# Attention and two routed expert layers on one core: scores of two head groups in turns, the second expert's weights fetched before the slot table

## The chip, the cores and the metric

One core of a Trainium2 chip runs the whole program in one launch. The metric is the device time of one execution in microseconds (us). Five engines work side by side, each through its own instructions in order: TensorE (PE; its weight loads are PEld), VectorE (DVE), ScalarE (ACT), GpSimd (POOL) and SyncE (SP), which here issues nearly all DMAs.

## The reference

Attention over 4 sequences, 8 heads, 768 positions, 64 dimensions; each query sees the first `n_global` = 8 keys and a causal window of `n_local` = 96, with a per-head distance penalty. Its output, 3072 rows of 512, goes through two layers of 8 experts with one expert per row:

```
scores = q @ k.T / 8 - slope[h] * dist ; a = softmax(where(keep, scores, -1e9)) ; x = a @ v
layer 1: e = argmax(x @ w_gate);             y = p[e] * relu(x @ w1[e]) @ w2[e]
layer 2: e = argmax(y @ w_gate2 + bias[mod]); the same with its own weights
```

Each expert has `w1` of 512x1024 and `w2` of 1024x512 in f32, 4 MB together.

## The kernel before

**Order of work.** Every piece of work is a function put at a time on a list (`Timeline.at`); the list is sorted once when the program is built, and so the order of instructions on each engine is fixed. The times are units of order alone: an attention tile is 4 units, a quarter of an expert slot is 1.

**Attention.** 24 tiles of 128 queries (`u`), 6 per sequence. All f32 operands are split in a high f16 and a low bf16 part, and a product is three matmuls. Heads go in four groups of two (`HEADS`, L237): (0,2) and (4,6) lie in partitions 0 to 63 of the transposed q and k, (1,3) and (5,7) in 64 to 127. For each group `g` come, in order: `score` (L589: 12 matmuls of 64 rows into one PSUM bank of tag A, 6 in the first tile of a sequence), two `rowmax` on VectorE (L608), two `expo` on ScalarE (L620), `etrans` (L625: f32 transposes on TensorE), `e_hi` (ScalarE) and `e_lo` (VectorE), then `pv` (12 matmuls). Tag A has two banks, so scores of one group can be written while those of the other are read. Beside this run the loads and transposes of the next tiles' q and k, and the routing of finished tiles: gate logits, the largest of 8, a position, and an indirect DMA that writes the row into its expert's region (`xs`).

**Expert layers.** Rows are worked in slots of 128 rows of one expert. Each slot has four quarters `p`: `mm1` (24 matmuls), a split of the result on ScalarE and VectorE (`mm1_out`), `mm2` (6 matmuls of 512 columns). At tile 15 the fullest expert is chosen as leader (`choose(0)`); its weights are loaded during the attention and split into f16 and bf16 (`split`: ScalarE L120, VectorE L347), and two slots of its rows start before the routing has ended. After the last tile, VectorE counts all rows and writes a table of slots (`slot_table`, L722): for each slot its base row, whether weights change there, and the next expert (FNXT). SyncE reads it with register loads (`val`, L804). In this input expert 0 leads; slots 0 and 1 finish it, and experts 1 to 7 begin at slots 2, 6, 9, 13, 16, 20 and 24 (counts computed from the reference).

**Weights and branches.** There is one set of f32 staging buffers, `st1[p]` and `st2[p]`. `stage_in` (L332) issues the DMAs; `change` (L892) splits them on ScalarE and VectorE under a branch; `refill` (L899) loads the next expert behind the splits, under a branch of SyncE on FNXT (L905), four pieces per slot. In layer 1, for slots after 17, each piece has a second register and a second branch (L909, FREFB), which loads the leader of layer 2 once the last expert has begun. The first weights after the leader's are loaded when the table is there (L1040). A SyncE branch that is not taken still raises the semaphores of the DMAs that it leaves out, after waiting for their earlier value, so a split of new weights cannot start before SyncE has passed every refill piece placed ahead of it.

Of the kernel before, what the change touches and what calls it, by code (L numbers as in the profile page):

```python
# [38 lines left out]
PICK = (15, 17)  # L39

MORE = (5, 2)
VHI = H * (D + 1)


# [6 lines left out]
}  # L51
ENG = {
    "kh": "P", "vh": "P", "qh": "P", "mh": "P", "ml": "P", "pp": "P", "pf": "V", "po": "V", "wa": "V",
# [47 lines left out]
def kernel(  # L101
# [199 lines left out]
    def constants():  # L301
        nc.vector.tensor_copy(out=rowoff_b, in_=rowoff[0:1, :])
        nc.vector.memset(meta[:, :, 0:NM - E], 0.0)
        nc.vector.memset(meta[:, :, 2:3], 1.0)
        nc.vector.tensor_copy(out=meta[:, :, 1], in_=tok_id)
        nc.vector.tensor_copy(out=mod_f[:, 1], in_=mod_i[:, :, 0])
        nc.vector.tensor_scalar(out=mod_f[:, 0], in0=mod_f[:, 1], scalar1=-1.0, scalar2=1.0, op0=ALU.mult, op1=ALU.add)
        for i in range(2):
            nc.vector.tensor_tensor(out=mod_b[:, i], in0=mod_f[:, i].unsqueeze(2).to_broadcast([128, NU, E]),
                                    in1=bias_sb[:, i].unsqueeze(1).to_broadcast([128, NU, E]), op=ALU.mult)  # L310
        nc.vector.tensor_tensor(out=meta[:, :, NM - E:NM], in0=mod_b[:, 0], in1=mod_b[:, 1], op=ALU.add)
        for m in range(2):
            nc.vector.tensor_copy(out=wg_hl[m][0], in_=wg_sb[m])
            nc.vector.tensor_tensor(out=wg_hl[m][1], in0=wg_sb[m], in1=wg_hl[m][0], op=ALU.subtract)

        nc.vector.tensor_scalar(out=late[:, 0:1], in0=slot_id, scalar1=float(PICK[1] + 1), scalar2=None, op0=ALU.is_equal)
        nc.vector.tensor_scalar(out=late[:, 1:2], in0=slot_id, scalar1=float(PICK[1] + 1), scalar2=None, op0=ALU.is_gt)

    def clear(m, e):

# [174 lines left out]
    def choose(m):  # L495

        cn = counts(m)
        mx = small.tile([128, 8], F32, tag="cmx", name="cmx", bufs=1)
        nc.vector.max(out=mx, in_=cn)
        ix = small.tile([128, 8], U32, tag="cix", name="cix", bufs=1)  # L500
        nc.vector.max_index(out=ix, in_max=mx, in_values=cn)
        nc.vector.tensor_copy(out=lead_f[m], in_=ix[:, 0:1])
        k = lead_k[m]
        ro = small.tile([1, 1], F32, tag="ro", name="ro", bufs=1)
        ts = nc.gpsimd.tensor_scalar
        if m == 0:
# [12 lines left out]
        if m == 1:  # L519
            nc.gpsimd.tensor_copy(out=lead_i[m][:, 3:4], in_=k[0:1, :])  # L520
        lead[m] = [nc.values_load(lead_i[m][0:1, i:i + 1], engines=[ET.SP], min_val=0,
                                  max_val=(E - 1, (E - 1) * REG + 128, E * REG - 128)[i]) for i in range(3)]


    vg_of = {}
# [62 lines left out]

    def score(u, g):  # L589

        d = st[u]
        p0 = 64 * (HEADS[g][0] % 2)
        sp = d["sp", g] = bank("A", "sp").rearrange("p (j c) -> p j c", j=2)
        keys = [(slice(WB - 128, WB), d["kt"], 0)]
        if u % QT:
            keys.append((slice(0, NA), kt_of[u - 1], 128 - LMAX + 1))
        else:
            keys[0] = (slice(0, 128), d["kt"], 0)
        for j, h in enumerate(HEADS[g]):
            for cols, kt, c0 in keys:  # L600
                for n, (x, y) in enumerate(((0, 0), (0, 1), (1, 0))):
                    lq = d["qt"][p0:p0 + 64, x, h // 2, :]
                    rk = kt[p0:p0 + 64, y, h // 2, c0:c0 + cols.stop - cols.start]
                    nc.tensor.matmul(out=sp[:, j, cols], lhsT=lq.bitcast(BF16) if x else lq,  # L604
                                     rhs=rk.bitcast(BF16) if y else rk, start=(n == 0), stop=(n == 2),
                                     skip_group_check=True)

    def rowmax(u, g, j):  # L608

# [107 lines left out]
            wide_attention()  # L717


    FBASE, FCHG, FNXT, FREFB, FCNT, FE1, NF = 0, 1, 2, 3, 4, 5, 6  # L720

    def slot_table(m):  # L722

# [7 lines left out]
        left, fin, lst, f = T("left", 1), T("fin", 1), T("lst", 1), T("f", NF)  # L731
        io = iota8[0:32, :]

        def col(i):
# [34 lines left out]
        def changes():  # L769

            stt(out=tmp, in0=start, scalar=slot_id, in1=sel, op0=ALU.is_equal, op1=ALU.mult)
            stt(out=tmp, in0=tmp, scalar=1.0, in1=not0, op0=ALU.mult, op1=ALU.mult, accum_out=first)
            stt(out=tmp, in0=start, scalar=s_end, in1=some, op0=ALU.is_equal, op1=ALU.mult, accum_out=has)

            stt(out=tmp, in0=tmp, scalar=first, in1=io, op0=ALU.mult, op1=ALU.mult, accum_out=col(FNXT))
            stt(out=tmp, in0=start, scalar=c0, in1=some, op0=ALU.is_equal, op1=ALU.mult)
            stt(out=tmp, in0=tmp, scalar=1.0, in1=io, op0=ALU.mult, op1=ALU.mult, accum_out=col(FE1))
            if m == 0:

                tt(out=fin, in0=col(FCNT), in1=slot_id, op=ALU.is_equal)  # L780
                tt(out=lst, in0=live, in1=has, op=ALU.subtract)
                tt(out=col(FCHG), in0=first, in1=fin, op=ALU.add)
                stt(out=fin, in0=first, scalar=late[:, 1:2], in1=late[:, 0:1], op0=ALU.mult, op1=ALU.add)
                tt(out=col(FREFB), in0=fin, in1=lst, op=ALU.mult)
            else:
                V.tensor_copy(out=col(FCHG), in_=first)
                V.memset(col(FREFB), 0.0)

        def turn():
            tpp = bank("C", "tpp")  # L790
            nc.tensor.transpose(tpp[0:NF, 0:32], f, ident[0:32, 0:32])
            tab[m] = const.tile([NF, 32], I32, name=f"slots{m}")
            V.tensor_copy(out=tab[m], in_=tpp[0:NF, 0:32])
            regs["e1", m] = val(m, FE1, 0, [ET.SP], E - 1)

        return lead_part, starts, bases, changes, turn

# [101 lines left out]
    def refill(m, s, k, i):  # L899

        if k == 0 and i == 0:
            regs["r", m, s] = (val(m, FNXT, s, [ET.SP], E - 1),
                               val(m, FREFB, s, [ET.SP], 1) if m == 0 and s > PICK[1] else None)
        nxt, refb = regs["r", m, s]
        with tc.If(nxt > 0):  # L905
            for p in (2 * k, 2 * k + 1):
                stage_in(p, m, nxt, (i,))
        if refb is not None:
            with tc.If(refb > 0):  # L909
                for p in (2 * k, 2 * k + 1):  # L910
                    stage_in(p, 1, lead[1][0], (i,))
        if k == 1 and i == 1:
            del regs["r", m, s]

# [93 lines left out]
    def refills(tl, m, s, n, t_min=-1e9):  # L1008
        for i in range(2):
            for k in range(2):  # L1010
                tl.at(max(n + MOFF[f"f{i}{k}"], t_min + 0.25 + 0.1 * k + 0.01 * i), lambda k=k, i=i: refill(m, s, k, i))

    def later(f):

        def guard(fn):
# [6 lines left out]
    def slots(tl, m, t0, t_table):  # L1022
# [14 lines left out]
        end = t1 + NP * fixed  # L1037
        assert t1 + MOFF["e1"] > t_table
        for p in range(NP):
            tl.at(t1 + MOFF["e1"] + 0.1 + 0.5 * p, lambda p=p: stage_in(p, m, regs["e1", m]))  # L1040
            for k in range(2):
                tl.at(t1 + MOFF["e1"] + 0.2 + 0.8 * p + 0.3 * k, lambda p=p, k=k: change(m, 0, p, 0, k))
                tl.at(t1 + MOFF["e1"] + 0.8 + 0.9 * p + 0.3 * k, lambda p=p, k=k: change(m, 0, p, 1, k))
# [52 lines left out]
    for u in range(NU):  # L1096
# [11 lines left out]
                       ("wa", lambda u: place_a(0, st[u], eng_of("wa"))), ("place", route_p)):  # L1108
            tl.at(SOFF.get(f"{nm}{u}", n + off_of(u, nm)), lambda u=u, fn=fn: fn(u))
        for g in range(4):  # L1110
            for nm, fn in (("S", score), ("EH", e_hi), ("EL", e_lo), ("PV", pv)):
                tl.at(n + g + OFF[nm], lambda u=u, g=g, fn=fn: fn(u, g))
            for nm, fn in (("R", rowmax), ("X", expo), ("T", etrans)):
                for j in range(2):
                    tl.at(n + g + OFF[f"{nm}{j}"], lambda u=u, g=g, j=j, fn=fn: fn(u, g, j))
# [62 lines left out]
```

## Time and profile before

| | |
|---|---|
| time, median of 3 runs | 887.59 us (887.04 to 899.56) |
| the profiled execution | 892.53 us, span 891.0 us |
| PE / PEld busy | 830.5 us (93%) / 632.3 us (71%) |
| DVE / ACT / POOL busy | 476.9 (54%) / 401.9 (45%) / 305.9 us (34%) |
| attention at its pace, 54.5 to 226 us | PE 168.23 us of 171.50, DVE 153.62, ACT 141.26 |
| first tiles, 22 to 54 us | PE 31.72 us of 32.00, but 275 matmuls against 557 in 34.48 us later |

Times in the trace are us from the start of the span. Attention fills the first quarter, to about 238 us with its last routing; layer 1 runs to about 600 us, layer 2 to the end. Busy times are of instructions as recorded; matmuls overlap, so that a group's busy time is less than count times mean.

### The profile page before, as it was taken

To read this page: it belongs to the slowest core of one execution; us is meant where nothing else is said; L and a number is where in the kernel's file an instruction comes from. 1 tells how busy PE (TensorE), PEld (TensorE's weight loads), DVE (VectorE), ACT (ScalarE), POOL (GpSimd) and SP (SyncE) were. 2 spreads that over 40 slices of the span, in tenths; PEclk is the share of its full clock that TensorE was granted. 3 is DMA by queue.
4 is the path that set the end of the run, shared out by engine and by line. 5 is a ranking of instruction groups with operands and counts; after the bars stand their busy time and mean duration, and the time that the engine had idled before them with its cause. 6 is when DMAs were issued, how large, how long until landed. Compare 5 with 4: busy or idle time off the path is not lost. (4 is left out here: it accounts for less than half of the span.)

```text
span 891.0 us, 30257 instructions
## 1 busy us (share of the span) xinstructions
PE 830.5 (93%) x10153; PEld 632.3 (71%) x10153; DVE 476.9 (54%) x1745; ACT 401.9 (45%) x858; POOL 305.9 (34%) x495
## 2 busy tenths in 40 slices
PE   5999999999688999999999788969999999999995
PEld 4888888888566777677777566647677777777773
DVE  5668898899843747656573634646311125111133
ACT  5568888888513434525341524332222225222242
POOL 6358777785432333423341422102111111111110
PEclk9999999999699999999999899999999999999998
DMA  8657766677249989987887684832562117322200
GB/s 145 177 150 211 181 147 144 155 193 226 66 104 267 248 185 240 221 262 181 248 240 168 148 216 135 213 116 52 150 162 69 52 50 209 78 62 52 51 28 16
DMA packets 227582, 133.99 MB, mean 150 GB/s; under 512 B 177148, under 2 KB 199676, under 8 KB 227360
## 3 DMA queue, kind: packets, MB, share of 16 engines
q1 hardware_dynamic: 220896, 112.10, 51.5%
q0 software_dynamic: 6320, 19.37, 6.2%
q8 instruction: 85, 1.39, 0.7%
q14 instruction: 137, 1.12, 0.4%
q10 hardware_dynamic: 144, 0.00, 0.0%
HBM read 79.54 MB, written 33.77 MB: 127 GB/s over the span
## 5 line engine op out<-in xcount | busy, mean ns | idle before, releaser
L870 PE MATMUL hp<-mx,h 128*128 128x128 f16 x3520 | 326.4, 222 | 9.6 <-ACTq L896 7.7
L870 PE MATMUL hp<-mx,l 128*128 128x128 f16 x1760 | 312.8, 222 | 7.0 <-DVEq L896 3.9
L870 PEld LDWEIGHTS <-h 128*128 128x128 f16 x3520 | 278.9, 99 | 48.7 <-ACTq L896 10.6
L881 DVE SCALAR_TENSOR_TENSOR hl<-hp,hh 128x256 bf16<-128x256 f32 x220 | 93.1, 423 | 268.7 <-ACT hh L880 139.4
L880 ACT ACTIVATE hh<-hp 128x256 f16<-128x256 f32 x220 | 84.2, 383 | 272.0 <-PE hp L870 233.8
L870 PEld LDWEIGHTS <-l 128*128 128x128 bf16 x1760 | 174.6, 99 | 8.8 <-DVEq L896 4.6
L889 PE MATMUL y<-l,hh 128*128 128x512 bf16 x440 | 167.5, 381 | 1.4 <-DVEq L896 1.4
L889 PE MATMUL y<-h,hh 128*128 128x512 f16 x440 | 167.7, 381 | 0.0
L889 PE MATMUL y<-h,hl 128*128 128x512 f16 x440 | 167.3, 380 | 0.0
L347 DVE TENSOR_TENSOR l<-st,h 128x1024 bf16<-128x1024 f32 x88 | 111.9, 1273 | 52.3 <-ACTq L896 25.3
L889 PEld LDWEIGHTS <-hh 128*128 128x128 f16 x880 | 77.4, 98 | 53.3 <-issue 0.8
L120 ACT CAST h<-st 128x1024 f16<-128x1024 f32 x88 | 91.2, 1043 | 50.7 <-SPq L909 20.7
L934 POOL DMA_INDIRECT out_dram<-o,ti x26 | 27.0, 1040 | 227.3 <-ACTq L896 189.9
L479 POOL DMA_INDIRECT xs<-r,posi x29 | 33.3, 1150 | 176.2 <-DVEq L896 61.3
L623 ACT ACTIVATE e<-e,nm 128x232 f32<-128x232 f32 (+1 forms) x192 | 84.0, 470 | 7.3 <-DVE nm L616 5.1
L889 PEld LDWEIGHTS <-hl 128*128 128x128 bf16 x440 | 43.2, 98 | 54.1 <-issue 2.2
L604 PE MATMUL sp<-kt,qt 64*128 64x128 f16 (+3 forms) x1056 | 77.8, 225 | 2.5 <-DVE nm L616 1.9
L604 PEld LDWEIGHTS <-qt 64*128 64x128 f16 (+1 forms) x1056 | 61.8, 101 | 14.5 <-issue 11.1
L616 DVE CUSTOM_DVE_ANT_0 e<-sp,bias_mid 128x232 f32<-128x232 f32 x160 | 61.3, 385 | 5.7 <-PE sp L604 5.6
L646 DVE TENSOR_TENSOR el<-et,eh 128x512 bf16<-128x512 f32 (+1 forms) x96 | 60.9, 634 | 1.7 <-ACT eh L640 1.7
L640 ACT CAST eh<-et 128x512 f16<-128x512 f32 (+1 forms) x96 | 52.4, 546 | 19.0 <-PE et L634 17.3
L634 PE MATMUL et<-ident,e 128*128 128x128 f32 x192 | 50.7, 297 | 1.0 <-ACT e L623 1.0
(201 smaller groups left out, 1138.9 us busy)
## 6 DMA issues: line engine op xcount, KB each, us to landing
st<-in_moe_w_dram SPq DMA_DIRECT2D x88, 512.0 KB
mxf<-xs SPq DMA_DIRECT2D x29, 266.0 KB
x_d<-r SPq DMA_DIRECT2D x29, 256.0 KB
ld_k<-in_k_dram SPq DMA_DIRECT2D x24, 256.0 KB
ld_q<-in_q_dram SPq DMA_DIRECT2D x24, 256.0 KB
ld_v<-in_v_dram SPq DMA_DIRECT2D x24, 256.0 KB
row<-xg SPq DMA_DIRECT2D x24, 256.0 KB
xs<-empty SPq DMA_DIRECT2D x18, 266.0 KB
```

Source lines behind the costliest of these rows:

```text
L120: nc.scalar.copy(out=out, in_=in_)
L347: (nc.vector if engines[i][1] == "V" else nc.gpsimd).tensor_tensor(out=l, in0=w, in1=h, op=ALU.subtract)
L604: nc.tensor.matmul(out=sp[:, j, cols], lhsT=lq.bitcast(BF16) if x else lq, rhs=rk.bitcast(BF16) if y else rk, start=(n == 0), stop=(n == 2 ...
L616: nc.vector.tensor_tensor_reduce(out=d["e", g][:, j, 0:w], in0=d["sp", g][:, j, 0:w], in1=(bias_mid if t else bias_first)[:, HEADS[g][j], ...
L623: nc.scalar.activation(out=e, in_=e, func=ACTF.Exp, bias=d["nm", g][:, j:j + 1], scale=-1.0)
L634: nc.tensor.transpose(tp[:, j, :], e[:, j, NA if t else 0:WB if t else 128], ident)
L640: nc.scalar.copy(out=eh[:, 0:n], in_=d["et", g][:, 0:n])
L646: nc.vector.tensor_tensor(out=el[:, 0:n], in0=d["et", g][:, 0:n], in1=d["eh", g][:, 0:n], op=ALU.subtract)
L870: nc.tensor.matmul(out=hp[:, j, :], lhsT=w[p][:, c, fs], rhs=r.bitcast(BF16) if x else r, start=(n == 0), stop=(n == 11))
L880: nc.scalar.activation(out=hh, in_=hp, func=ACTF.Relu)
L881: nc.vector.scalar_tensor_tensor(out=hl, in0=hp, scalar=0.0, in1=hh, op0=ALU.max, op1=ALU.subtract)
L889: nc.tensor.matmul(out=d["y"], lhsT=d[hx, p][:, j, :], rhs=w[p][:, j, :], start=(p == 0 and j == 0 and i == 0), stop=(p == NP - 1 and j == ...
```

## The change

There are two parts. **Scores**: `score(u, g)` is called for even `g` alone and writes two groups into both banks of tag A, matmul by matmul in turns from partitions 0 to 63 and 64 to 127. The odd group's rowmax goes 0.6 units earlier than before, its expo 0.3. **Weights**: `choose(0)` also writes a guess of the next expert (1 if the leader is 0, else 0), and `stage_in` loads it right behind the leader's splits; when the table is there, a branch per quarter (`first_next`) loads again where the guess was wrong. The second branch of `refill` and its register are gone for slots below AHEAD = 21; from 21 on FNXT = 8 stands for the leader of layer 2, in two branches inside the first.

```diff
+AHEAD = PICK[1] + 4
...
+    "c0s": 1.3, "c1": 15.6, "c1s": 2.0, "rl": 10.6, "oddR": 0.6, "oddX": 0.3, "oddT": 0.0,
...
-        nc.vector.tensor_scalar(out=late[:, 0:1], in0=slot_id, scalar1=float(PICK[1] + 1), scalar2=None, op0=ALU.is_equal)
+        nc.vector.tensor_scalar(out=late[:, 0:1], in0=slot_id, scalar1=float(AHEAD), scalar2=None, op0=ALU.is_equal)
...
+        else:
+            ts(out=lead_i[m][:, 3:4], in0=lead_f[m][0:1, :], scalar1=0.0, scalar2=None, op0=ALU.is_equal)
...
     def score(u, g):
-        p0 = 64 * (HEADS[g][0] % 2)
-        sp = d["sp", g] = bank("A", "sp").rearrange("p (j c) -> p j c", j=2)
+        sp = [bank("A", "sp").rearrange("p (j c) -> p j c", j=2) for _ in range(2)]
+        for i in range(2):
+            d["sp", g + i] = sp[i]
...
-        for j, h in enumerate(HEADS[g]):
+        for j in range(2):
             for cols, kt, c0 in keys:
                 for n, (x, y) in enumerate(((0, 0), (0, 1), (1, 0))):
+                    for i in range(2):
+                        h = HEADS[g + i][j]
+                        p0 = 64 * (h % 2)
...
-                tt(out=col(FREFB), in0=fin, in1=lst, op=ALU.mult)
+                tt(out=fin, in0=fin, in1=lst, op=ALU.mult)
+                stt(out=col(FNXT), in0=fin, scalar=float(E), in1=col(FNXT), op0=ALU.mult, op1=ALU.add)
+                ts(out=spec, in0=lead_f[m][0:32, :], scalar1=0.0, scalar2=None, op0=ALU.is_equal)
+                tt(out=spec, in0=col(FE1), in1=spec, op=ALU.subtract)
+                ts(out=col(FMORE), in0=spec, scalar1=0.0, scalar2=None, op0=ALU.max)
...
     def refill(m, s, k, i):
         if k == 0 and i == 0:
-            regs["r", m, s] = (val(m, FNXT, s, [ET.SP], E - 1),
-                               val(m, FREFB, s, [ET.SP], 1) if m == 0 and s > PICK[1] else None)
+            regs["r", m, s] = val(m, FNXT, s, [ET.SP], E if m == 0 and s >= AHEAD else E - 1)
...
         with tc.If(nxt > 0):
-            for p in (2 * k, 2 * k + 1):
-                stage_in(p, m, nxt, (i,))
-        if refb is not None:
-            with tc.If(refb > 0):
...
+            if m == 0 and s >= AHEAD:
+                with tc.If(nxt < E):
+                    stage(m, nc.s_assert_within(nxt, 0, E - 1, skip_runtime_bounds_check_because="it is under E here"))
+                with tc.If(nxt > E - 1):
+                    stage(1, lead[1][0])
+            else:
+                stage(m, nxt)
...
+    def first_next(m, p):
+        if m == 1:
+            stage_in(p, m, regs["e1", m])
+        else:
+            with tc.If(regs["e1", m] > 0):
+                stage_in(p, m, val(m, FE1, 0, [ET.SP], E - 1))
...
-            tl.at(t1 + MOFF["e1"] + 0.1 + 0.5 * p, lambda p=p: stage_in(p, m, regs["e1", m]))
+            tl.at(t1 + MOFF["e1"] + 0.1 + 0.5 * p, lambda p=p: first_next(m, p))
...
-            for nm, fn in (("S", score), ("EH", e_hi), ("EL", e_lo), ("PV", pv)):
+            if g % 2 == 0:
+                tl.at(n + g + OFF["S"], lambda u=u, g=g: score(u, g))
+            for nm, fn in (("EH", e_hi), ("EL", e_lo), ("PV", pv)):
...
+                    t = n + g + OFF[f"{nm}{j}"] - (OFF[f"odd{nm}"] if g % 2 else 0)
...
+            tl.at(max(MOFF["split0"] + 1.3 * i + p + 1.2, 100 + 0.05 * (2 * p + i)), lambda p=p, i=i: stage_in(p, 0, lead[0][3], (i,)))
```

## Rows read from the trace of the kernel before

**Rows 1.** Busy time of each engine in four full attention tiles; header: columns.

```profile
core 0: us, PE busy (x) PEld busy (x) DVE busy (x) ACT busy (x) POOL busy (x), PEclk, DMA share, GB/s
...
142.34:176.82 34.48, 34.48 (x557) 30.58 (x556) 30.64 (x139) 29.51 (x63) 26.06 (x39) 1.00 0.62 145
```

**Rows 2.** TensorE in order of time: start, us, line, operands, shape, count.

```profile
143.81 0.22 PE L661 MATMUL xp<-vs,eh 128*128 128x65 f16 x2
143.88 0.19 PE L661 MATMUL xp<-vs,el 128*128 128x65 f16 x1
144.00 0.78 PE L604 MATMUL sp<-kt,qt 64*128 64x128 f16 x12
144.71 0.33 PE L633 MATMUL et<-ident,e 128*128 128x128 f32 x1
```

**Rows 3.** Groups by line, same four tiles: count, busy us, mean ns, idle.

```profile
L604 PE MATMUL sp<-kt,qt 64*128 64x128 f16 (+1 forms) x192 | 12.5, 212 | 0.0
L616 DVE CUSTOM_DVE_ANT_0 e<-sp,bias_mid 128x232 f32<-128x232 f32 x32 | 12.3, 385 | 0.0
```

**Rows 4.** TensorE in order of time, the first tiles.

```profile
31.57 1.34 PE L604 MATMUL sp<-kt,qt 64*128 64x128 f16 x12
...
46.52 1.34 PE L604 MATMUL sp<-kt,qt 64*128 64x128 f16 x12
...
54.55 0.33 PE L633 MATMUL et<-ident,e 128*128 128x128 f32 x1
```

**Rows 5.** TensorE in order of time, after its waits; brackets: idle before, releaser.

```profile
265.14 0.27 PE L870 MATMUL hp<-mx,h 128*128 128x128 f16 x2 [0.81 <-DMA mx<-mxs]
...
285.62 0.28 PE L870 MATMUL hp<-mx,h 128*128 128x128 f16 x2 [1.58 <-ACTq L896]
286.90 0.29 PE L870 MATMUL hp<-mx,l 128*128 128x128 f16 x1 [0.99 <-DVEq L896]
...
494.32 0.29 PE L870 MATMUL hp<-mx,h 128*128 128x128 f16 x2 [4.19 <-ACTq L896]
495.59 0.29 PE L870 MATMUL hp<-mx,l 128*128 128x128 f16 x1 [0.99 <-DVEq L896]
...
549.03 0.28 PE L870 MATMUL hp<-mx,h 128*128 128x128 f16 x2 [1.06 <-ACTq L896]
```

**Rows 6.** ScalarE in order of time, weight casts behind their waits.

```profile
284.48 1.04 ACT L120 CAST h<-st 128x1024 f16<-128x1024 f32 x1 [6.88 <-SPq L905]
...
493.17 1.04 ACT L120 CAST h<-st 128x1024 f16<-128x1024 f32 x1 [7.42 <-SPq L909]
...
547.89 1.04 ACT L120 CAST h<-st 128x1024 f16<-128x1024 f32 x1 [4.99 <-SPq L909]
```

**Rows 7.** Busy time of each engine by stretch, columns as in rows 1.

```profile
236.00:256.00 20.00, 15.02 (x174) 11.71 (x174) 15.98 (x84) 3.91 (x11) 5.11 (x7) 0.85 0.11 42
266.00:284.00 18.00, 18.00 (x210) 12.84 (x207) 4.21 (x14) 3.27 (x10) 3.45 (x8) 1.00 1.05 292
287.00:290.00 3.00, 3.00 (x24) 2.52 (x24) 2.42 (x6) 2.47 (x5) 1.86 (x4) 0.51 1.62 160
495.60:501.50 5.90, 5.90 (x39) 3.94 (x40) 4.64 (x11) 5.07 (x9) 1.96 (x4) 0.50 0.49 135
```

**Rows 8.** SyncE queue in order of time: DMA issues.

```profile
266.00 0.39 SPq L334 DMA_DIRECT2D st<-in_moe_w_dram  x1
...
275.04 0.37 SPq L338 DMA_DIRECT2D st<-in_moe_w_dram  x1
...
482.66 1.40 SPq L847 DMA_TRANSPOSE mx<-mxs  x1
486.64 0.36 SPq L940 DMA_DIRECT2D x_d<-r  x1
...
493.14 1.25 SPq L945 DMA_TRANSPOSE x2t<-x_d  x1
```

**Rows 9.** VectorE in order of time, the end of the slot table.

```profile
253.05 0.21 DVE L783 SCALAR_TENSOR_TENSOR tb_fin<-tb_first,late 32x1 f32<-32x1 f32 x1
```

More of the change, by code (lines that the diff above doesn't have):

```diff
@@ L314, in constants @@
             nc.vector.tensor_tensor(out=wg_hl[m][1], in0=wg_sb[m], in1=wg_hl[m][0], op=ALU.subtract)
-        nc.vector.tensor_scalar(out=late[:, 0:1], in0=slot_id, scalar1=float(PICK[1] + 1), scalar2=None, op0=ALU.is_equal)
-        nc.vector.tensor_scalar(out=late[:, 1:2], in0=slot_id, scalar1=float(PICK[1] + 1), scalar2=None, op0=ALU.is_gt)
+        nc.vector.tensor_scalar(out=late[:, 0:1], in0=slot_id, scalar1=float(AHEAD), scalar2=None, op0=ALU.is_equal)
+        nc.vector.tensor_scalar(out=late[:, 1:2], in0=slot_id, scalar1=float(AHEAD), scalar2=None, op0=ALU.is_gt)
     def clear(m, e):
@@ L520, in choose @@
             nc.gpsimd.tensor_copy(out=lead_i[m][:, 3:4], in_=k[0:1, :])
+        else:
+            ts(out=lead_i[m][:, 3:4], in0=lead_f[m][0:1, :], scalar1=0.0, scalar2=None, op0=ALU.is_equal)
         lead[m] = [nc.values_load(lead_i[m][0:1, i:i + 1], engines=[ET.SP], min_val=0,
-                                  max_val=(E - 1, (E - 1) * REG + 128, E * REG - 128)[i]) for i in range(3)]
+                                  max_val=(E - 1, (E - 1) * REG + 128, E * REG - 128, 1)[i])
+                   for i in range(3 if m else 4)]
     vg_of = {}
@@ L598, in score @@
             keys[0] = (slice(0, 128), d["kt"], 0)
-        for j, h in enumerate(HEADS[g]):
+        for j in range(2):
             for cols, kt, c0 in keys:
                 for n, (x, y) in enumerate(((0, 0), (0, 1), (1, 0))):
[L602 to L606, printed above, removed]
+                    for i in range(2):
+                        h = HEADS[g + i][j]
+                        p0 = 64 * (h % 2)
+                        lq = d["qt"][p0:p0 + 64, x, h // 2, :]
+                        rk = kt[p0:p0 + 64, y, h // 2, c0:c0 + cols.stop - cols.start]
+                        nc.tensor.matmul(out=sp[i][:, j, cols], lhsT=lq.bitcast(BF16) if x else lq,
+                                         rhs=rk.bitcast(BF16) if y else rk, start=(n == 0), stop=(n == 2),
+                                         skip_group_check=True)
     def rowmax(u, g, j):
@@ L717, in widen @@
             wide_attention()
-    FBASE, FCHG, FNXT, FREFB, FCNT, FE1, NF = 0, 1, 2, 3, 4, 5, 6
+    FBASE, FCHG, FNXT, FMORE, FCNT, FE1, NF = 0, 1, 2, 3, 4, 5, 6
     def slot_table(m):
@@ L730, in slot_table @@
         cur, s_end, s_n, first, has = T("cur", 1), T("s_end", 1), T("s_n", 1), T("first", 1), T("has", 1)
-        left, fin, lst, f = T("left", 1), T("fin", 1), T("lst", 1), T("f", NF)
+        left, fin, lst, spec, f = T("left", 1), T("fin", 1), T("lst", 1), T("spec", 1), T("f", NF)
         io = iota8[0:32, :]
@@ L783, in changes @@
                 stt(out=fin, in0=first, scalar=late[:, 1:2], in1=late[:, 0:1], op0=ALU.mult, op1=ALU.add)
-                tt(out=col(FREFB), in0=fin, in1=lst, op=ALU.mult)
+                tt(out=fin, in0=fin, in1=lst, op=ALU.mult)
[3 more added lines that the diff above has]
+                ts(out=col(FMORE), in0=spec, scalar1=0.0, scalar2=None, op0=ALU.max)
             else:
                 V.tensor_copy(out=col(FCHG), in_=first)
-                V.memset(col(FREFB), 0.0)
+                V.memset(col(FMORE), 0.0)
         def turn():
@@ L793, in turn @@
             V.tensor_copy(out=tab[m], in_=tpp[0:NF, 0:32])
-            regs["e1", m] = val(m, FE1, 0, [ET.SP], E - 1)
+            regs["e1", m] = val(m, FMORE if m == 0 else FE1, 0, [ET.SP], E - 1)
         return lead_part, starts, bases, changes, turn
@@ L901, in refill, with stage @@
         if k == 0 and i == 0:
-            regs["r", m, s] = (val(m, FNXT, s, [ET.SP], E - 1),
-                               val(m, FREFB, s, [ET.SP], 1) if m == 0 and s > PICK[1] else None)
-        nxt, refb = regs["r", m, s]
-        with tc.If(nxt > 0):
-            for p in (2 * k, 2 * k + 1):
-                stage_in(p, m, nxt, (i,))
-        if refb is not None:
-            with tc.If(refb > 0):
-                for p in (2 * k, 2 * k + 1):
-                    stage_in(p, 1, lead[1][0], (i,))
+            regs["r", m, s] = val(m, FNXT, s, [ET.SP], E if m == 0 and s >= AHEAD else E - 1)
+        nxt = regs["r", m, s]
+        def stage(m, e):
+            for p in (2 * k, 2 * k + 1):
+                stage_in(p, m, e, (i,))
+        with tc.If(nxt > 0):
+            if m == 0 and s >= AHEAD:
[5 more added lines that the diff above has]
+                stage(m, nxt)
         if k == 1 and i == 1:
@@ L1114 @@
                 for j in range(2):
-                    tl.at(n + g + OFF[f"{nm}{j}"], lambda u=u, g=g, j=j, fn=fn: fn(u, g, j))
+                    t = n + g + OFF[f"{nm}{j}"] - (OFF[f"odd{nm}"] if g % 2 else 0)
+                    tl.at(t, lambda u=u, g=g, j=j, fn=fn: fn(u, g, j))
         for i in range(2):
```

1 row of the table OFF is left out of this document.

## The prediction

> **What bounds the kernel now.** I read the busy time by stretch first. In four full attention tiles TensorE is busy for all of 34.48 us, VectorE for 30.64, ScalarE for 29.51, GpSimd for 26.06 [rows 1]: 8.62 us a tile, set by TensorE, with VectorE next at 30.64/4 = 7.66. Whatever is taken off TensorE there is gained only until VectorE sets the pace. The timeline of TensorE then shows the scores' share. Twelve matmuls are busy for 0.78 us [rows 2], the last one 0.21 of that [rows 3], so they start (0.78 - 0.21)/11 = 52 ns apart: they stream one behind the other. The next transpose starts 0.71 us after the first, where 12 x 52 = 0.62, so leaving costs 0.09; entering takes 0.12 where one `pv` matmul follows another in 0.07/2 = 35 ns, so about 0.085 more [rows 2]. Together 0.175 us a group, four times a tile.
>
> The first tiles look the same but slower: the same twelve take 1.34 us instead of 0.78, and one tile takes 46.52 - 31.57 = 14.95 us, until the transposes have their short 0.33 us again at 54.55 [rows 4]. That is TensorE at the lower of its two levels, 1.2 instead of 2.4 GHz, though it hardly pauses.
>
> In the expert layers TensorE works without a break but for waits. The ones that matter here are at changes of weights: 1.58 + 0.99 us at 285.62, 4.19 + 0.99 at 494.32, 1.06 at 549.03 and one more like it at 586.67 [rows 5]. The timeline of ScalarE says what they stand on: its first cast of the new weights waits 6.88, 7.42 and 4.99 us, each time for a SyncE branch [rows 6]. The data aren't late, SyncE is late in skipping a `refill` piece. Behind the two longest waits the granted clock is 0.51 and 0.50, the lower level, for 3.0 and 5.9 us of full work [rows 7].
>
> **Part 1, scores in turns.** No matmul is added or removed; the order changes. Two groups at a time halve the changes between 64-row scores and 128-row work: 2 x 0.175 = 0.35 us less a tile. What two matmuls from different halves cost next to each other no row shows. The upper bound is the present 52 ns (they follow each other), the lower one the 35 ns in which `pv` matmuls of 65 columns, each with new weights, follow each other. I take 35: nothing in the scores' rows but streaming sets the 52, and the halves share no rows of the array; above 52 I see no reason, since no column is added. A pair of groups then costs 24 x 35 = 0.84 instead of 1.25 us, a tile 0.82 less, and TensorE's tile is 8.62 - 0.35 - 0.82 = 7.45 (8.27 if nothing runs at once). That is under VectorE's 7.66, so VectorE becomes the bound, without losing any work of its own.
>
> The new wait is that a pair of scores takes both banks of tag A and so waits for all four rowmax of the pair before: about 4 x 0.385 = 1.5 us [rows 3]. Between two pairs TensorE has 7.45/2 - 0.84 = 2.9 us of other work in its queue, so the banks are free in time if VectorE starts at once; what stands behind the waiting scores is the transposes and `pv` of older groups, and ScalarE and VectorE wait for those. The moved rowmax and expo cost nothing themselves. With VectorE at 7.66 and ScalarE at 7.38 of work, I don't expect 7.66: three in-order engines at nearly equal load wait for each other. I put the tile halfway, at 8.14, and save 0.48 (bounds 0 and 0.96). At full speed there are 17 such tiles and 3 with half the scores, where VectorE has less to do and I take 0.7: 17 x 0.48 + 3 x 0.7 = 10.3 us.
>
> At the lower clock TensorE is far behind the others, and the whole saving counts. By doubling (2 x 0.82 + 0.35 to 0.7) a tile loses 2.0 to 2.3 of its 14.95; from 20 to 54.5 us there are 34.5/14.95 = 2.3 tiles, so about 5 us, if the clock rises at the same time.
>
> The Trainium skill (TensorEngine Tiling (Array Packing), PSUM Bottleneck) warns that tiling speeds up TensorE but not the emptying of PSUM, which may become the bottleneck. Taken strictly it leaves nothing here beyond what VectorE has free; that is the second rival below, by which the attention gains 3 us. The trace of before agrees so far that VectorE has only a ninth of its time free [rows 1].
>
> **Part 2, the weights.** Eight DMAs of 512 KB (4.2 MB) move from 266.00 to 275.04 [rows 8] to about 242 to 250, behind the last row's DMA on SyncE. There the DMA engines are 0.11 busy; at the 292 GB/s of the later stretch [rows 7] 4.2 MB take 14 us, to about 256, just when the rows of slot 0 are asked for. If those queue behind, the 0.81 us wait at 265.14 [rows 5] grows by up to 3; I take none and keep 3 for the range. In this input the leader is expert 0 and the next is 1, so the guess holds, and four skipped branches replace the eight issues: in 482.66 + 1.40 to 486.64 four skips fit 2.58 us [rows 8], 0.65 each at most, so 2.6 us of SyncE's queue replace 9.4. The row transposes queued behind come 7 us earlier, and so does the skip for which ScalarE waits. The stall at 285 goes: 1.58 + 0.99, and 3.0 x 0.49 = 1.5 for the clock, 4.1 us.
>
> Fewer branches: between slot 18's first piece and the release at 493.17, SyncE no longer does five skips and two register loads. At 0.5 us each (bounds 0, if it waits elsewhere instead, and 0.65) it comes 3.5 us earlier. TensorE's 4.19 becomes 0.7, its 0.99 for VectorE's half of the split stays, and the lower clock behind it (5.9 x 0.5 = 2.95) doesn't come after so short a wait: about 6.4 us. The two later changes lose a register load and some skips a slot: 1.5 us together.
>
> Against it: four more dependent operations of 0.21 us [rows 9] ahead of the table, which slot 0's rows wait for: 0.8 us. The new operation in `choose(0)` costs nothing: GpSimd is idle for a quarter of the attention [rows 1]; without that cover it would be one short operation.
>
> **The sum.** 10.3 + 5 + 4.1 + 6.4 + 1.5 - 0.8 = 26.5 us. The profiled execution took 892.53 us (span 891.0 and 1.5 around it), so 866.0; the median of the runs is 4.9 lower, and the same step from 887.59 gives 861.1, say 861.
>
> **Rivals.** First, the halves don't run at once. For it: no row shows it. Then a full tile saves 0.35, 20 tiles 7.0, the first tiles 0.35 to 0.7 x 2.3, about 1.2; with 11.2 from part 2 it makes 19.4, 868.
>
> Second, VectorE and ScalarE take the gain back: with 12% idle they leave a tile 0.96 at most, and the four rowmax in a row come in bursts. The attention then gains 3 in place of 15.3: 873. Against it: the slack of 2.9 - 1.5 us above.
>
> Third, the stalls at new weights come back one piece later, since ScalarE still waits for a skipped branch of every slot: part 2 gives 2 in place of 12, so 870.
>
> Fourth, on the other side: the clock stays at the lower level through the attention, or falls there, now that TensorE has pauses behind VectorE. For it: the first 54 us show that hardly pausing is not enough. Against it: with the present mix it is 1.00 all through four tiles [rows 1], and the packed scores leave it just as busy while it is slow. Price: a tile of 14.95 - 2.2 = 12.75 instead of 8.62, 4.1 more. From 4 more tiles at that level the 16.2 us of the other terms (5 + 11.2) are gone; from 9 on it is over 2% slower; all 17 full tiles, and 3 that cost about 3 more each, make 887.6 + 79 - 16.2 = 950.
>
> Fifth, the clock rises earlier, because TensorE's columns come denser: two of the slow tiles at 8.14 instead of 12.75 give 9 more, 852.
>
> **Chances.** Forecast 0.41 (853 to 868 by itself), no concurrency 0.12, gain taken back 0.15, stalls return 0.13, lower clock 0.05, earlier rise 0.14. The forecast's low end takes VectorE's floor (8 more), its high end the 3 us of queued rows and a smaller first term. 846 to 877 leaves out the fourth case and the ends of the others. A measurement of this kernel tells about 2% from no change, 17.8 us: faster is below 869.8, slower above 905.3. Faster: 0.40 + 0.14, most of the first rival (0.08) and some of the third (0.05) = 0.67; slower 0.05; the rest 0.28.
>
> **What would show it.** Right: score groups of 24 in 0.85 us or less between two transposes, VectorE above 0.93 busy, tiles near 8.1; no wait of over 0.5 us at slot 2, one of under 1 at slot 20 with the clock at 1.00 behind it; eight weight DMAs near 245 us. Wrong: 24 scores in 1.25 us; tiles of 8.5 with TensorE waiting for rowmax; scores still at the slow pace after 60 us; ScalarE's casts at slots 2 or 20 again waiting over 5 us for SyncE.

## The result and the profile after

| kernel | median us (all runs) | ratio to before, 95% interval |
|---|---|---|
| before | 890.43 (887.04 to 899.56) | |
| after | 856.17 (854.7 to 861.0) | 0.961 [0.952, 0.970] |

The forecast was 861 in 846 to 877. The profiled execution of the changed kernel took 856.3 us (span 854.7), the one of before 892.53: 36.2 us apart (36.3 in the spans), where the sum had 26.5. Ratios are taken over undisturbed executions alone, so they need not be the quotient of the medians.

How far the changed kernel is ahead at the same piece of work, from the starts in the two traces:

| TensorE starts | before | after | ahead by |
|---|---|---|---|
| attention tile 4 | 58.7 | 43.9 | 14.8 |
| attention tile 23 | 217.8 | 191.3 | 26.5 |
| first front slot | 238.9 | 213.4 | 25.5 |
| slot 0 | 265.1 | 242.4 | 22.7 |
| behind the change of weights at slot 2 | 291.1 | 264.1 | 27.0 |
| behind slots 20 and 21 | 512.4 | 483.6 | 28.8 |
| four slots later, behind the change to expert 7 | 566.4 | 529.4 | 37.0 |

The waits for a new expert's weights fall in the last quarter of the slot ahead of its first one. So what this text and the expectations call slot 2 and slot 20 are, by the count of `hp` matmuls (96 a slot), slots 1 and 19: 275.7 to 291.1 and 481.8 to 500.8 us before.

First the busy time by stretch, of the changed kernel: the four tiles that answer to [rows 1], the slow stretch in tile 19, the change of weights at slot 2 and the one at slot 20, which answer to [rows 7].

```profile
core 0: us, PE busy (x) PEld busy (x) DVE busy (x) ACT busy (x) POOL busy (x), PEclk, DMA share, GB/s
119.60:150.70 31.10, 29.09 (x558) 25.52 (x558) 30.05 (x141) 28.39 (x64) 25.91 (x39) 1.00 0.68 163
...
162.20:169.00 6.80, 6.38 (x68) 5.42 (x68) 3.26 (x17) 3.17 (x7) 3.91 (x8) 0.50 0.86 205
...
253.00:264.10 11.10, 11.00 (x135) 8.06 (x136) 6.04 (x16) 6.20 (x10) 2.23 (x5) 1.00 0.42 99
...
464.80:470.50 5.70, 3.09 (x34) 2.01 (x35) 3.24 (x7) 4.13 (x6) 3.92 (x5) 1.00 0.66 151
```

A tile takes 31.10/4 = 7.78 us instead of 8.62. TensorE works 7.27 of them and is no longer busy throughout; VectorE is at 0.97. Next the scores, in groups by line over the same four tiles (answers to [rows 3]) and in TensorE's order of time (answers to [rows 2, 4]).

```profile
L626 DVE CUSTOM_DVE_ANT_0 e<-sp,bias_mid 128x232 f32<-128x232 f32 x32 | 11.8, 383 | 0.0
L614 PE MATMUL sp<-kt,qt 64*128 64x128 f16 (+1 forms) x193 | 6.5, 212 | 0.0
```

```profile
23.18 1.34 PE L614 MATMUL sp<-kt,qt 64*128 64x128 f16 x23 [0.62 <-DVE nm L626]
28.81 0.89 PE L614 MATMUL sp<-kt,qt 64*128 64x128 f16 x24
...
112.61 0.78 PE L614 MATMUL sp<-kt,qt 64*128 64x128 f16 x24
113.32 0.44 PE L644 MATMUL et<-ident,e 128*128 128x128 f32 x2
```

One score still takes 212 ns from start to end, but 24 of them are done in the 0.78 us that twelve took, and in 6.5 us instead of 12.5 in all. The rows at 23.18 and 28.81 show the clock's rise at 29 us: the same 24 at 1.34, then at 0.89 us. (The clock column can't show it: it reads 1.00 up to a trace's first recorded level, here at 29.1 us.) Then TensorE behind its waits (answers to [rows 5]) and ScalarE's casts of new weights (answers to [rows 6]); the brackets hold the idle time before and its releaser.

```profile
162.62 1.11 PE L702 MATMUL xtp<-ident,row 128*128 128x128 f32 x4 [2.53 <-DMA row<-xg]
...
242.42 0.27 PE L885 MATMUL hp<-mx,h 128*128 128x128 f16 x2 [2.92 <-DMA mx<-mxs]
...
466.43 0.29 PE L885 MATMUL hp<-mx,h 128*128 128x128 f16 x2 [1.67 <-ACTq L911]
467.70 0.23 PE L885 MATMUL hp<-mx,l 128*128 128x128 f16 x1 [0.98 <-DVEq L911]
480.77 0.23 PE L885 MATMUL hp<-mx,l 128*128 128x128 f16 x1 [1.80 <-DVE l L349]
```

```profile
255.37 1.04 ACT L122 CAST h<-st 128x1024 f16<-128x1024 f32 x1 [0.49 <-DVE hl L896]
...
465.28 1.04 ACT L122 CAST h<-st 128x1024 f16<-128x1024 f32 x1 [2.30 <-DVEq L911]
...
478.92 1.04 ACT L122 CAST h<-st 128x1024 f16<-128x1024 f32 x1 [1.97 <-SPq L924]
...
510.63 1.04 ACT L122 CAST h<-st 128x1024 f16<-128x1024 f32 x1 [2.93 <-SPq L924]
```

No wait is left at slot 2, at slot 20 1.67 of 4.19 us, and ScalarE waits 2 to 3 us for SyncE where it waited 5 to 7. New are 2.53 us in the attention from 160.1 on, with 6.8 us of low clock behind it, and 2.92 us at slot 0 where 0.81 stood. Last, the queues behind slot 0's wait: SyncE's (answers to [rows 8]) and GpSimd's.

```profile
216.35 0.41 SPq L336 DMA_DIRECT2D st<-in_moe_w_dram  x1
...
220.10 2.80 SPq L340 DMA_DIRECT2D st<-in_moe_w_dram  x2
233.27 5.45 SPq L846 DMA_DIRECT2D mxf<-xs  x3
```

```profile
219.89 0.99 POOL L481 DMA_INDIRECT xs<-row,posi  x1 [2.01 <-DMA xs<-row,posi]
...
227.40 0.99 POOL L481 DMA_INDIRECT xs<-row,posi  x1 [5.54 <-DMA xs<-row,posi]
```

The weights go out at 216 to 223 as planned (242 to 250 in the forecast, and everything here is 25 us earlier). The last scatter of attention rows waits 5.54 us for the scatter ahead of it, and the rows of slot 0 (`mxf`), which read what it writes, are asked for at 233.27.

### The profile page after: what moved, and what is told of

It reads as the page before. It is cut to its first block, busy times and chain, and to the rows that moved or that the text cites. A ratio compares the mean times of both kernels' runs of the same rounds, so it can differ in the third digit from the quotient of the medians.

```text
span 854.7 us, 30054 instructions
## 1 busy us (share of the span) xinstructions
PE 781.2 (91%) x10045; PEld 595.1 (70%) x10153; DVE 471.1 (55%) x1749; ACT 396.7 (46%) x858; POOL 304.6 (36%) x496
## 5 line engine op out<-in xcount | busy, mean ns | idle before, releaser
L904 PE MATMUL y<-l,hh 128*128 128x512 bf16 x332 | 126.1, 380 | 0.2 <-DVEq L911 0.2
L954 POOL DMA_INDIRECT out_dram<-o,ti x26 | 27.1, 1042 | 226.8 <-ACTq L911 191.0
L633 ACT ACTIVATE e<-e,nm 128x232 f32<-128x232 f32 (+1 forms) x192 | 80.8, 468 | 3.6 <-DVE nm L626 2.5
L626 DVE CUSTOM_DVE_ANT_0 e<-sp,bias_mid 128x232 f32<-128x232 f32 x160 | 59.0, 383 | 0.6 <-PE sp L614 0.5
L644 PE MATMUL et<-ident,e 128*128 128x128 f32 x192 | 49.1, 290 | 1.7 <-ACT e L633 1.3
L643 PE MATMUL et<-ident,e 128*128 128x128 f32 x160 | 44.3, 302 | 1.8 <-DVE rs L678 1.2
L671 PEld LDWEIGHTS <-eh 104*128 104x128 f16 (+1 forms) x704 | 44.1, 101 | 2.1 <-ACT h L122 0.7
```

The lines of the kernel that those rows point to most:

```text
L626: nc.vector.tensor_tensor_reduce(out=d["e", g][:, j, 0:w], in0=d["sp", g][:, j, 0:w], in1=(bias_mid if t else bias_first)[:, HEADS[g][j], ...
L633: nc.scalar.activation(out=e, in_=e, func=ACTF.Exp, bias=d["nm", g][:, j:j + 1], scale=-1.0)
L643: nc.tensor.transpose(tp[:, 2 + j, :], e[:, j, 0:128], ident)
L644: nc.tensor.transpose(tp[:, j, :], e[:, j, NA if t else 0:WB if t else 128], ident)
L904: nc.tensor.matmul(out=d["y"], lhsT=d[hx, p][:, j, :], rhs=w[p][:, j, :], start=(p == 0 and j == 0 and i == 0), stop=(p == NP - 1 and j == ...
```

## The experiments

The theory after the comparison: the two halves of the partitions run at once and VectorE then sets the tile; the clock rises earlier because of it; slot 2 is won by the early weights, slots 20 to 24 by the fewer branches; the early weights cost slot 0 its late start and the registers of `choose(0)` the wait in tile 19. The rivals stand in the expectations. Times are medians with all runs; each ratio is to runs of before in the same session.

**One part alone, and the parts taken apart.**

```
scores_alone:   before.py + score(), odd offsets and their loop of the change
weights_alone:  the change - score(), odd offsets and their loop
one_half_then_other, in score():
-        for j in range(2): ...
-                    for i in range(2):      # halves in turns
+        for i in range(2):                  # all 12 of one half, then of the other
+            for j in range(2): ...
no_early_weights:
-            tl.at(max(...), lambda p=p, i=i: stage_in(p, 0, lead[0][3], (i,)))
+  first_next(): stage_in(p, m, regs["e1", m]) as before; no fourth register in choose(0)
```

> The kernel before with the scores' part of the change alone (two groups in one call, odd groups' steps placed earlier); branches and first next weights as before. Theory A, both parts work and add up: the attention keeps the whole of its gain, the first expert slot starts some 25 us earlier than before, and the stalls at slots 2 and 20 stay as long as before (15.4 and 19.0 us for these slots): about 864 us, ratio 0.970. Theory B, the earlier rise of the clock needs the whole change or was chance: about 873. Theory C, the scores' gain is given back in the experts: 880 or more.

Measured: 868.79 us (867.53 to 872.77), ratio 0.983 [0.978, 0.988]; profile 866.7. By the trace theory A: the first front slot starts at 212.7, as early as in the change, and slots 2 and 20 take 15.8 and 18.9 us. By the time it lies between A and B, since before ran at 886 in that session, below its profile of 891.0.

> The changed kernel with the scores' part put back to what it was before: branches and early weights alone. Theory A: slot 2 takes 11.1 us instead of 15.4, slot 20 14.8 instead of 19.0, the slots after it 3 to 7 us less together, slot 0 starts 2 to 3 us later against the front than before, and the attention is as long as before, with the clock rising at 54 us: about 878, ratio 0.986. Theory C, the weights' part works only because the attention ends earlier: 887 or more. Theory D, the weights' part also brings the clock up early: 868.

Measured: 880.25 us, but 866.44, 866.87, 880.25, 888.12 and 890.57 one by one; ratio 0.979 [0.974, 0.984], which is of the two at 866 alone. The trace (889.0) shows A's slots: 11.1 us at slot 2 and 14.3 at slot 20. What makes two levels of time needed a run of its own (below).

> The changed kernel with the 24 scores of a pair issued one group after the other (first all of one half of the partitions, then all of the other) instead of in turns; all offsets as changed. Theory A, the halves run at once and that is the gain of a warm tile: 24 scores take 1.2 us instead of 0.7, TensorE has 1.0 us more in each tile and comes back level with VectorE: tiles of 8.3 to 8.6 us instead of 7.8, some 10 us slower than the change, 866. Theory B, the gain comes from the fewer switches and the earlier steps of the odd groups: 856 to 858. If the early rise of the clock needs the halves at once, 10 us more in either case.

Measured: 863.79 us (861.93 to 867.36), ratio 0.976 [0.971, 0.981], 8 us slower than the change. TensorE in order of time, and its busy time in four tiles that answer to the four above:

```profile
117.88 1.22 PE L614 MATMUL sp<-kt,qt 64*128 64x128 f16 x24
```

```profile
125.80:158.30 32.50, 31.84 (x558) 28.66 (x558) 29.93 (x141) 27.91 (x63) 25.80 (x38) 1.00 0.67 154
```

Theory A as to the cause: taken out of turns, 24 scores need 1.22 us, so the turns do run the halves at once. The tile is 8.13 us. So of the 0.84 us that a warm tile gained, 0.35 are the halves at once, and 0.49 came without that, from the pairing and the earlier steps of the odd groups. The clock rose at 30.8 here too.

> The changed kernel with the first next expert's weights staged after the slot table as before; the fewer branches stay. Theory A, slot 2's gain is the early weights and slot 0's late start is their price: slot 2 takes 15 us again (4 more), slot 0 starts 2.3 us earlier against the front since the last scatter of rows no longer queues among the weights, and tile 19's stall of 2.5 us may go with the fourth register: between 853 and 859, slots 20 to 24 as in the change. Theory B, slot 2's gain came from the fewer branches: slot 2 stays at 11.1 and the time falls to 851.

Measured: 856.01 us (853.88 to 857.81), ratio 0.968 [0.964, 0.972]; profile 852.3. Neither sum was right alone: slot 2 and the one behind it take 14.0 and 12.8 us (11.1 and 11.3 in the change), so that gain is the early weights'; slot 0 is only 1.1 us earlier; and tile 19 takes 8.4 instead of 11.3 us. GpSimd and SyncE without the early weights:

```profile
223.35 0.98 POOL L481 DMA_INDIRECT xs<-row,posi  x1 [1.65 <-DMA xs<-row,posi]
```

```profile
230.99 5.04 SPq L844 DMA_DIRECT2D mxf<-xs  x3
```

The last scatter goes out 4.05 us earlier, the rows 2.3. Slots 20 to 24 stay as in the change: those are the fewer branches. By the times of the same session these are worth 868.79 - 856.01 = 12.8 us, while the early weights win 4.4 us at slot 2 and lose about as much at slot 0 and in tile 19. No net gain of theirs can be measured (0.968 against 0.961, the intervals overlap).

**The wait in tile 19.**

```
+        if m: lead_regs(m)                              # end of choose(m)
+    tl.at(78.3, lambda: lead_regs(0))                   # was 75.4, inside choose(0)
```

> The changed kernel with one move: SyncE reads the leading expert's four registers behind the skipped row transfer and the two loads of that tile instead of ahead of them. Theory A, the 2.5 us wait of TensorE at 159.9 and the low clock from 162.2 to 169.0 come from SyncE, which in the changed kernel reads a fourth register there (0.58 us more, 2.9 us for all four) before it signals the row: the wait falls under 0.5 us, the clock stays at 2.4 GHz, tile 19 takes 8 instead of 11.3 us, some 3 us faster, about 853. Theory B, another step is late there next (GpSimd's, or the weights' first piece): no difference.

Measured: 853.19 us (851.15 to 856.33), ratio 0.959 [0.955, 0.964]; profile 849.4. TensorE in order of time, and SyncE's signal of the row of a later tile:

```profile
160.76 0.66 PE L707 MATMUL xtp<-ident,row 128*128 128x128 f32 x4 [0.71 <-DMA row<-xg]
```

```profile
178.00 0.09 SPq L700 DMA_DIRECT2D row<-xg  x1
```

Theory A, at that place: 0.71 us instead of 2.53, no low clock from 162 on, tile 19 in 7.5 us. But the first weights are now ahead of the row of a later tile, which VectorE had ended at 177.10 and SyncE signals at 178.00, and TensorE waits 1.28 us there; tile 23 is 1.8 us ahead of the change instead of 3. It is the fastest of the kernels, by less than the intervals tell apart. The fourth register is only part of the wait: in the change SyncE signals that row 1.83 us after VectorE ended it, in `scores_alone`, where three registers are read ahead of it, still 1.29 us after, and there tile 19 takes 9.5 us.

**Does VectorE set the warm tile?**

```
vectore_relieved (on the change):  fin_s() left out; fin_r(): reciprocal(out=rs, in_=d["xp", i][:, :, D:D + 1])
                                   "pf": "V" -> "P", "po": "V" -> "P"
no_add (on registers_later):       fin_s() left out, as above
rows_later (on registers_later):   "rt": 10.0 -> 10.15, "rh": 10.25 -> 10.3
rows_later_no_add:                 both
```

> The changed kernel with less for VectorE: the addition of 1e-9 ahead of the reciprocal is left out (the sums are at least 1), and the one-hot of the chosen expert and the conversion of its index are moved to GpSimd: some 0.6 us less VectorE in each tile. Theory A, VectorE sets the pace of the warm tiles (32.5 of 34.0 us): tiles of 7.3 to 7.5 us instead of 7.85, 8 to 10 us faster, about 847. Theory B, TensorE with its waits for the rows sets it: 1 us or less. Theory C, GpSimd (28.7 of 34.0 us and two more steps in its queue) becomes late for the placing: slower.

Measured: 857.83 us (855.65 to 859.45), ratio 0.963 [0.959, 0.968]. Not A: from the start of tile 9 to that of tile 18 it takes 70.7 us, the change 68.6, before 76.6 (74.9 in its second profile, below). In time it can't be told from the change (0.963 against 0.961), so nothing was won and a loss is not shown.

> The base (registers read later, 853.2 us) with only the addition of 1e-9 ahead of the reciprocal left out, two of VectorE's steps of 0.07 us each in a tile (24 tiles, 3.4 us in all); nothing is moved to GpSimd. Theory B, VectorE alone sets the pace: 2.5 to 3.4 us faster, 850. Theory A, the ring of waits: under 2 us. If it grows slower, as the kernel with the lighter VectorE did, GpSimd's two further steps were not what made that one slow.

Measured: 861.48 us (859.06 to 862.27), ratio 0.972 [0.966, 0.977]: slower, with nothing moved to GpSimd. Part of it is the clock, low again at 34.0, 122.7 and 187.6 for 3.4 us each; but tiles 9 to 12, at 2.4 GHz throughout, take 31.8 us instead of 30.5 too. (Four traces of the change's tiles lie between 30.4 and 30.6; the two profiles of before, 33.8 and 32.9, warn that one trace can be 0.8 off.)

> The changed kernel with the registers read later (as in the run registers_later, 853.2 us, which is the base here) and with the four transposes of a finished row placed behind the next pair of scores on TensorE instead of ahead of it. Theory A, what sets a warm tile is a ring of two queues that are worked in order: VectorE's row ends late, TensorE's transposes wait for it 0.3 to 1.0 us, and the scores that VectorE needs next stand behind them; with the scores ahead, that wait is gone and the tile falls to VectorE's own 7.5 to 7.6 us, 3 to 6 us faster, 848 to 850. Theory B, VectorE alone sets it (32.5 of 34.0 us busy): within 1.5 us of 853. Theory C, the row is now late for what follows it: slower.

Measured: 863.14 us (856.16 to 866.7), ratio 0.973 [0.966, 0.979]: slower than its base; tiles 9 to 17 take 71.5 us, in the base 68.6.

> Both edits on the base (transposes of a row behind the next scores; addition left out). Theory A and theory B alike expect the sum of the two; A 844 to 848, B 849 to 851. With it the best of the kernels so far, if either edit helps.

Measured: 858.63 us (856.73 to 865.54), ratio 0.970 [0.964, 0.976]. Not the sum of two gains, since neither edit gains.

TensorE's longest waits in 78 to 136 us (total, times, longest), of the change, of `no_add` and of `rows_later`, and busy time in 82 to 106 us of the same three (the base, `registers_later`, reads as the change does: 4.8 us of waits, VectorE 22.84):

```profile
PE xtp L702 <- DMA row<-xg: 4.8, 7, 1.0
```

```profile
82.00:106.00 24.00, 21.85 (x421) 19.13 (x421) 22.85 (x107) 21.04 (x47) 19.61 (x29) 1.00 0.66 155
```

```profile
PE xtp L706 <- DMA row<-xg: 7.3, 7, 1.9
```

```profile
82.00:106.00 24.00, 21.45 (x417) 18.88 (x417) 21.99 (x99) 20.20 (x45) 19.64 (x29) 1.00 0.66 154
```

```profile
PE sp L619 <- DVE nm L631: 3.3, 8, 1.0
```

```profile
82.00:106.00 24.00, 22.55 (x428) 19.86 (x425) 23.35 (x106) 20.33 (x47) 20.09 (x29) 1.00 0.67 155
```

Less work on VectorE gave a less busy VectorE (22.85 to 21.99 us) and a longer wait of TensorE for its rows. That these are waits for VectorE, and not for a transfer, the order of time shows, here one row of the change and then one of before:

```profile
92.97 0.42 DVE L692 TENSOR_TENSOR row<-xp,rs 128x256 f32<-128x256 f32 x1
93.41 0.10 SPq L695 DMA_DIRECT2D row<-xg  x1
93.54 0.66 PE L702 MATMUL xtp<-ident,row 128*128 128x128 f32 x4 [0.74 <-DMA row<-xg]
```

```profile
119.49 0.42 DVE L682 TENSOR_TENSOR row<-xp,rs 128x256 f32<-128x256 f32 x1
119.94 0.09 SPq L685 DMA_DIRECT2D row<-xg  x1
120.73 0.53 PE L692 MATMUL xtp<-ident,row 128*128 128x128 f32 x3
```

VectorE ends the row, SyncE passes the transfer (which is left out here) 0.03 us later, and in the change TensorE starts 0.11 to 0.14 us after that. So it goes in 14 of the 15 rows from 93 to 203 us; the other is the one of tile 19. Before, TensorE came to these rows 0.13 to 0.81 us after SyncE. In the change, then, TensorE follows the end of VectorE's rows; when a row ends is not the same as how much VectorE has to do. With the rows moved out of the way, that wait is gone and the scores wait for the rowmax of the pair before instead: the wait that the prediction named and costed at nothing. So VectorE's load alone is not what sets the tile, and neither is that one wait; theories A and B both failed on the times. That the tile follows from how several in-order queues stand against each other fits the four runs, but none of them shows it; what would shorten the tile stays open.

**Where the clock rises.**

```
heated_before, on before.py:
+    wz = const.tile([128, 512], BF16, name="wz")       # ones
+    def heat(n): n times matmul(out=bank("D", "wz"), lhsT=wz[:, 0:128], rhs=wz, ...)
+    for t, n in [(-50, 7), (-5.2, 2), (-3.9, 2), (-2.3, 2), (-1.6, 2)] + [(0.2 + g, 1) for g in range(8)]:
+        tl.at(t, lambda n=n: heat(n))
```

> The kernel before with 23 extra matmuls of 128x512 on TensorE while it waits for its first loads and between the steps of the first two tiles; nothing else is changed and their result is not used. Theory A, the first tiles of the kernel before are slow because the granted clock is low until 54 us, and the price of that is what the change won beyond the forecast: if the clock rises before 30 us, tile 4 starts at 43 to 47 us instead of 58.7 and the time falls by 10 to 14 us, about 876. Theory B, the low clock follows the mix of work in the first tiles: the clock rises at 54 us again and the time grows by the extra matmuls, 2 to 6 us.

Measured: 893.21 us (883.26 to 898.17), ratio 1.003 [0.998, 1.008]. The clock rose at 36.0, and from tile 2 to tile 4 it took 17.3 us instead of 27.1: the price of a late rise is real, 10 us here against the first profile of before (5 against the second, below, where these tiles take 22.2 us). The tile that begins at 176 and most of the next then ran at the lower level, 0.50 from 176.0 to 196.5 us, after TensorE had been busy 3.11 of the 4 us before, and took 24.9 us instead of 16.5. On the total theory A failed, though its condition, a rise before 30 us, was not met either.

> The kernel of weights_alone once more (the old scores with the new branches and the early weights), whose five times lay at 866 twice and at 880 to 891 three times, with a profile of one of 889. Theory A, with the old scores the clock can rise early too, and the times of 866 are such executions: an execution of about 866 shows the clock at 2.4 GHz before 40 us, and tile 4 some 10 us earlier. Theory B, the early rise needs the scores in pairs: the clock rises at 54 to 58 us in any execution, and the two levels of time come from a later place.

Measured: 873.59 us (868.42 to 888.63), ratio 0.986 [0.976, 0.996]; profile 866.9.

> The kernel before, unchanged, profiled once more. Theory A, where its clock rises differs between executions (29 to 58 us) and so do its times (878 to 899 us). Theory B, it rises at 54 us again and the spread comes from later stretches of low clock, as the ones of 176 to 205 us in two other kernels with the old scores.

Measured: 885.39 us (880.57 to 897.22), ratio 1.001 [0.996, 1.006]; profile 879.1. Busy time and clock by stretch (columns as above) of `weights_alone`, `weights_alone_again` and `before_again`, all with the old scores:

```profile
30.00:42.00 12.00, 12.00 (x104) 10.52 (x103) 6.51 (x25) 6.33 (x13) 4.67 (x7) 0.50 0.64 176
43.00:54.00 11.00, 11.00 (x107) 9.58 (x105) 5.30 (x24) 5.21 (x12) 5.51 (x8) 0.50 0.51 138
```

```profile
30.00:42.00 12.00, 12.00 (x193) 10.65 (x192) 10.51 (x44) 10.43 (x23) 8.73 (x13) 1.00 0.87 238
```

```profile
30.00:42.00 12.00, 12.00 (x103) 10.25 (x101) 6.86 (x25) 6.37 (x14) 4.00 (x6) 0.50 0.67 182
43.00:54.00 11.00, 11.00 (x184) 9.76 (x184) 9.56 (x45) 8.99 (x20) 7.34 (x11) 1.00 0.56 152
```

The first profile of before over the same stretch:

```profile
30.00:42.00 12.00, 12.00 (x104) 10.47 (x103) 6.66 (x25) 6.33 (x13) 4.53 (x7) 1.00 0.66 176
```

TensorE is busy in all of them; 104 matmuls in 12 us are 1.2 GHz, 193 are 2.4. In the last row the clock column reads 1.00 all the same, since the first level on record in that trace begins at 54.4 us; that the kernel before ran at 1.2 GHz ahead of it is read from its pace, which is that of `weights_alone` at 0.50. Theory A in both: one and the same kernel has its clock up at 29.6 or 58.2 us, and before at 42.6 or 54.4. The nine profiles with the new scores have it up, for 40 us or more, from a point between 20.9 and 37.4. Four executions against nine make it likely that the new order brings the rise earlier; they don't show it, since the old one can do it too.

## Why the prediction was right, and where it was not

The right case happened together with most of the fifth rival, the early clock. Step by step:

**Halves at once: right, and cheaper.** I took 35 ns a matmul between 35 and 52. Starts in the trace come in pairs 3 to 4 ns apart, the pairs 43 to 63: (0.78 - 0.21)/23 = 25 ns. TensorE's tile is 7.27 instead of 7.45. The Trainium skill (TensorE: Matmul & The Clock Gate, Part 3, The mechanism and Measured speedup vs the span model) gives about 4 ns between the starts of matmuls in different row groups, and the trace agrees; by it my lower bound was too high.

**The warm tile: right in size, its reason not confirmed.** 8.14 was forecast, 7.78 came, VectorE at 0.97 as named: 0.84 us saved where 0.48 was put. From tile 4 to 23 that is 11.7 us against 10.3, although tile 19 gave some 3 back in a place that the prediction had at nothing: it covered the further operation in `choose(0)` on GpSimd and left out the further register, which SyncE reads ahead of a row that TensorE waits for. That 11.7 came so near to 10.3 is luck: two misses offset each other, and the profile of before is long here too. Its second profile takes 156.2 instead of 159.1 us from tile 4 to 23, which leaves 8.9. "VectorE becomes the bound" did not stand its tests as far as it means VectorE's load: TensorE does follow VectorE's rows, but the halfway house of 8.14 was a guess, and why the tile lies at 7.78 is open. More than half of the tile's gain (0.49 of 0.84) doesn't need the halves at once: it came from the pairing's fewer switches or from the moved steps of the odd groups, which I had at nothing; the runs don't part these two.

**First tiles: mis-sized.** 5 us forecast, "if the clock rises at the same time"; 14.8 in the traces. It rose 25 us earlier. Of the 14.8, 5.5 are no effect of the change: the second profile of before reaches tile 4 at 53.2. What the scores alone give is nearer 5: `weights_alone_again`, with the old scores and the rise at 29.6, reaches tile 4 at 47.9, 4.0 us behind the change with its rise at 29.1.

**Early weights: 4.1 forecast at slot 2, 4.3 came,** with the mechanism as told: no wait, no low clock, and it goes away without them. The 3 us that were kept for slot 0's rows came as well (2.1 us longer a wait, 2.8 us of lead), but not by the rows queuing: the scatter ahead of them goes out 4.05 us later. Without the early weights slot 0 starts only 1.1 us earlier. Another 0.6 us is TensorE's wait for the slot table with its four added operations (1.5 us, in `scores_alone` 0.9; 0.8 was forecast). The rest stays open.

**Fewer branches: right in kind, in the wrong slots.** 6.4 us were put at slot 20; slots 20 and 21 together gave 2.7, because after SyncE the next in the row were late, VectorE's half of the split (1.80 us at 480.77) and ScalarE behind VectorE (2.30 at 465.28). 1.5 us were put at the later ones, where 8.2 came. The wait that I hadn't costed there stood in the trace of before, in front of the second layer's logits:

```profile
529.06 0.19 PE L417 MATMUL lp<-wgh,x2t 128*128 128x8 f16 x1 [2.73 <-DMA x2t<-x_d]
```

3.4 us of low clock followed it, and that slot took 15.4 us, in the change 11.1: 4.3 of the 8.2. SyncE holds its transpose until the rows `x_d` have landed, and it had issued those behind the same branches. `scores_alone`, with the old branches, keeps the loss (16.0 us for that slot), `no_early_weights`, with the new ones, doesn't (11.1). Together 10.9 against 7.9 forecast, and 12.8 us by the times of `scores_alone` and `no_early_weights`.

**The rivals.** No concurrency: refuted by 1.22 against 0.78 us. Gain taken back: no, 11.7 us in the warm tiles, not 3. The Trainium skill's warning (TensorEngine Tiling (Array Packing), PSUM Bottleneck) that emptying PSUM may become the bottleneck did not take the gain back here: a full tile saved 0.84 of the 0.96 us that VectorE had left. The wait for rowmax exists once the rows are out of its way. Stalls return: half, at slots 20 and 21. Lower clock: one tile, 6.8 us. By the times of one session each, the scores' part alone is worth 1.7% (15 us, 15.3 forecast), the branches 13. That 15 meets 15.3 is partly luck: in the profile of `scores_alone` the clock rises at 29.7 us, which the forecast left out. The forecast's 26.5 sits 8 below the 34 of the medians because branches gave more and the clock rose early; part of the 8 is the kernel before itself, whose medians in the later sessions were 885.7 to 889.2.

## What to carry over

Before a difference of two profiles is explained, profile the kernel before a second time: two executions of it here differ by 12 us, and the two stretches that looked like the change's largest gains, the first tiles and the warm ones, were partly that. When an in-order queue is shortened, list everything that stands in it behind the removed instructions: the largest single gain of the fewer branches, 4.3 us, was at a transpose that no step had named. An engine at 97% is not thereby the bound; take a little of its work away and see whether the time follows. And where a column reads full clock, compare the pace of the same instructions.

## What the hardware did that was not expected

Full work didn't settle TensorE's level: in `weights_alone` it was busy for all of 30 to 42 and 43 to 54 us at 1.2 GHz, in `weights_alone_again`, the same program, for all of 30 to 42 us at 2.4. Two matmuls of 64 rows in different halves started 3 to 4 ns apart in spite of new weights for each. A scatter of 128 rows took until 7.5 us after its issue before the next one could go out (219.89 to 227.40) while the weights ran at 366 GB/s, and 4.3 us without them (219.03 to 223.35), at 63 GB/s; one execution of each.
